# A Winograd convolution with batch norm and SiLU: readers of a bank swapped, and the last unit's copies and turns put in another order

## The chip, the core and the metric

The kernel runs on one core of a Trainium2 chip. The metric is the device time of one execution in microseconds (us). The kernel before takes 195.81 us, the median of 3 runs (195.16 to 196.03).

The engines have these names in the profile: PE is TensorE (matmuls, with its weight loads as PEld), DVE is VectorE, ACT is ScalarE, POOL is GpSimd, and SP is SyncE, which here only issues DMAs. A "q" behind a name (ACTq, SPq) is that engine's sequencer, for example while it issues a DMA. The accumulators of PE lie in eight banks of 512 fp32 columns by 128 partitions; the kernel holds them all as one tile, `ps_all`.

## The reference

The input x is (2, 2048, 1024), the weights w are (3, 1024, 1024), all in bfloat16. A convolution with three taps along the sequence is followed by a batch norm with given mean and variance, and by SiLU.

```python
K = 3
P = K // 2
S = x.shape[1]
xp = jnp.pad(x, ((0, 0), (P, P), (0, 0)))
y = sum(jnp.einsum('bsc,cd->bsd', xp[:, k:k + S, :], w[k]) for k in range(K))
inv_std = 1.0 / jnp.sqrt(var + 1e-5)
y = (y - mean) * (g * inv_std) + b
return _silu(y)
```

## The kernel before, in words

The convolution is done in Winograd form: six outputs at a time are worked out from eight input rows. A sequence of 2048 has 342 such tiles (`NTB`). There are three kinds of work.

**Transforms** (`transform`, L209). PE multiplies windows of x with a small constant matrix `Rm` (L216), which gives eight planes j of transformed input, already turned so that channels lie on partitions. ACT (L230) or DVE (L232) casts a group of two, three or four such results from banks of `ps_all` into `T_sb` in SBUF. A running estimate of each engine's load (`load`, `EVAC`) chooses which of the two casts a group.

**Weights** (`scale_weights`, `pair_weights`). POOL adds and subtracts the three taps to make the planes' weights, `uch` (L160 to L162); ACT scales copies of the taps by 2 and 4 for it (L148). Planes 0 and 7 use the raw taps, `wch`.

**Units** (`unit`, L251). A unit is 128 output channels of one batch: 16 units, of 8 channel blocks by 2 batches. For each of the eight planes, eight matmuls (`mms`, L241) add up 1024 input channels into one of four banks, called A, B, C and G. The planes come in the order 1, 3, 2, 4, 5, 7, 6, 0. Planes 1 and 2 go to bank A, 3 and 4 to B, 5 and 6 to C, 7 to G and 0 again to A. A second plane is added on top of the first, so the first must be copied out before: ACT copies plane 1 to `m1`, the sum of 1 and 2 to `s1`, plane 3 to `m3`, the sum of 3 and 4 to `s2`, plane 5 to `m5` (`copy_out`, L280). DVE builds the differences and the six outputs y0 to y5 with `scalar_tensor_tensor` (`stt`, L273, and one plain add, L305). The difference d1 is 2 m1 - A; the differences of the other two pairs are written over a bank: 2 m3 - B over bank B, 2 m5 - C over bank G. Units use the banks 0 to 3 and 4 to 7 by turns.

The order of the code around the change is:

```python
        yield from mms(bA, 2, dc, bi, c0, c1, False)
        copy_out(s1, A)
        stt(d1, m1, 2.0, A, op1=ALU.subtract)
        yield from mms(bB, 4, dc, bi, c0, c1, False)
        copy_out(s2, B_)
        for i in (2, 4):
            stt(y[i], B_, ALPHA * 2.0 ** i, s1)
        stt(B_, m3, 2.0, B_, op1=ALU.subtract)
```

Each engine does its instructions in the order in which the program emits them. Where two instructions touch the same bank from different engines, the one that was emitted later waits for the earlier one, also where both only read.

At the end of a unit three SiLU activations (L317) are not run but put on a list, `late`. They write `yT`, the outputs of the unit with channels on partitions. The next unit runs them between its own copies: `pace` (1, 0, 1, 1, 0) says how many of the list are taken off ahead of the copies m1, m3, s1, s2 and m5. So ACT's order in a unit is SiLU of y2 and y4, m1, m3, SiLU of y1, y3 and y5, s1, SiLU of y0, s2, m5. The scaling of weights comes behind m5. After that, `finish` turns the outputs back with one DMA transpose on SP's queue (`turn`, L386) and issues the stores of the unit before (`store_unit`, L400 and L404).

**Unit 0** is interleaved with the transforms of the second batch: every group of transforms is followed by two or three of the unit's matmuls. The unit has banks 0 to 3, the transforms go round banks 4 to 7. ACT and DVE do the casts of T_sb and the copies and differences of the unit in one stream. Plane 7 comes first in this unit.

**The last unit** (unit 15) is done in two parts, so that the end is short: columns 0 to 245 (`cut`) and then columns 245 to 342. Part one uses banks 4 to 7. Within it, after plane 7 (48 matmuls), PE turns the outputs of unit 14 itself (18 transposes, L446), and ACT copies them out to `o_before` (three copies, L469), which are stored from SP's queue. Part two uses banks 0 to 3. Behind it, PE turns part one's outputs in two blocks of 128 and 117 columns, which DVE copies to `o_end0` and `o_end1` (L478), and then part two's 97 columns in three steps, each behind its SiLU; DVE copies these to `o_end2` in two pieces (L486). Then come the stores: the parts of the blocks whose rows are a multiple of 16 on SP's queue, two small remainders of 30 and 2 rows of 128 elements on ACT's queue (`store_block`, L454 and L457).

Of the kernel before, what the change touches and what calls it, by code (L numbers as in the profile page):

```python
# [9 lines left out]
ALU = mybir.AluOpType  # L10
FP32 = mybir.dt.float32
BF16 = mybir.dt.bfloat16
# [15 lines left out]
ALPHA = -1.0 / 20.0  # L28
BETA = -4.0 / 5.0
M_OUT = 6  # L30
NJ = 8
WT = 21

# [2 lines left out]
def kernel(  # L36
# [10 lines left out]
    nc = tc.nc  # L47
    B, S, C = x.shape
    D = w.shape[2]
    P = 128  # L50
    CT = C // P
    DC = D // P
    assert S % P == 0 and C % P == 0 and D % P == 0
    NTB = (S + M_OUT - 1) // M_OUT
    assert NTB <= 512
    NWIN = (NTB + WT - 1) // WT

    NB = (NTB + P - 1) // P
# [46 lines left out]
    for k in range(NJ):  # L105
        j = 1
        while j < 7:
# [5 lines left out]
            while j1 + 1 < 7 and BT[j1 + 1][k] == v:  # L113
# [3 lines left out]
                out=Rm[:, j:j1 + 1, :],  # L117
# [4 lines left out]
                op1=ALU.add,  # L122
            )
            j = j1 + 1
    for j in (0, 7):
        for k in range(NJ):
            if BT[j][k] != 0:
                nc.gpsimd.affine_select(
                    out=Rm[:, j, :],
                    in_=Rm[:, j, :],  # L130
                    compare_op=ALU.not_equal,
                    fill=float(BT[j][k]),
                    base=-k,
                    pattern=[[-M_OUT, WT]],
                    channel_multiplier=1,
# [58 lines left out]
    epool = ctx.enter_context(tc.tile_pool(name="epool", bufs=1))  # L194
# [39 lines left out]
    def mms(bk, j, dc, bi, c0, c1, start):  # L234

        for ct in range(CT):
            if j in (0, 7):
                lhsT = raw[dc][0 if j == 0 else 2][:, ct, :]
            else:
                lhsT = wts[dc][:, j - 1, ct, :]  # L240
            nc.tensor.matmul(  # L241
                ps_all[:, bk * 512:bk * 512 + c1 - c0],
                lhsT=lhsT,
                rhs=T_sb[bi][:, ct, j, c0:c1],
                start=start and ct == 0,
                stop=ct == CT - 1,
                skip_group_check=not start,
            )
            yield

    def unit(dc, bi, c0, c1, banks, yT, late, pace=(1, 0, 1, 1, 0), seven_first=False):  # L251

        nn = c1 - c0  # L260
        A, B_, C_, G = [ps_all[:, k * 512:k * 512 + nn] for k in banks]
        bA, bB, bC, bG = banks
        pace = list(pace)

        def et(name):
            return epool.tile([P, NTB], FP32, name=name)[:, 0:nn]

        m1, m3, m5, s1, s2, d1 = (et(n) for n in ("m1", "m3", "m5", "s1", "s2", "d1"))
        y_all = epool.tile([P, M_OUT, NTB], FP32, name="y")[:, :, 0:nn]
        y = [y_all[:, i] for i in range(M_OUT)]  # L270

        def stt(o, i0, s, i1, op1=ALU.add):
            nc.vector.scalar_tensor_tensor(out=o, in0=i0, scalar=s, in1=i1, op0=ALU.mult, op1=op1)  # L273
            load["dve"] += 0.0013 * nn

        def copy_out(dst, src):
            for _ in range(pace.pop(0)):
                if late:
                    late.pop(0)()
            nc.scalar.copy(dst, src)  # L280
            load["act"] += 0.0013 * nn

        if seven_first:
            yield from mms(bG, 7, dc, bi, c0, c1, True)
        yield from mms(bA, 1, dc, bi, c0, c1, True)
        copy_out(m1, A)
        yield from mms(bB, 3, dc, bi, c0, c1, True)
        copy_out(m3, B_)
        yield from mms(bA, 2, dc, bi, c0, c1, False)
        copy_out(s1, A)  # L290
        stt(d1, m1, 2.0, A, op1=ALU.subtract)
        yield from mms(bB, 4, dc, bi, c0, c1, False)
        copy_out(s2, B_)
        for i in (2, 4):
            stt(y[i], B_, ALPHA * 2.0 ** i, s1)
        stt(B_, m3, 2.0, B_, op1=ALU.subtract)
        yield from mms(bC, 5, dc, bi, c0, c1, True)
        copy_out(m5, C_)
        while late:
            late.pop(0)()  # L300
        for i in (1, 3, 5):
            stt(y[i], B_, ALPHA * 2.0 ** i, d1)
        if not seven_first:
            yield from mms(bG, 7, dc, bi, c0, c1, True)
        nc.vector.tensor_tensor(y[5], G, y[5], op=ALU.add)  # L305
        yield from mms(bC, 6, dc, bi, c0, c1, False)
        for i in (2, 4):
            stt(y[i], C_, BETA * 0.5 ** i, y[i])
        stt(G, m5, 2.0, C_, op1=ALU.subtract)
        yield from mms(bA, 0, dc, bi, c0, c1, False)  # L310
        for i in (1, 3, 5):
            stt(y[i], G, BETA * 0.5 ** i, y[i])
        stt(y[0], s2, ALPHA, A)
        stt(y[0], C_, BETA, y[0])

        def silu(i0, i1):
            nc.scalar.activation(  # L317
                yT[:, i0:i1:2, c0:c1],
                y_all[:, i0:i1:2],
                ACT.Silu,  # L320
                bias=beta[:, dc:dc + 1],
                scale=sk[:, dc:dc + 1],
            )

        late.extend(lambda i=i: silu(*i) for i in ((2, 5), (1, 6), (0, 1)))

    def run(gen, n=None):
        while n is None or n > 0:
            if next(gen, run) is run:
                return  # L330
            if n is not None:
                n -= 1

    units = [(dc, bi) for dc in range(DC) for bi in range(B)]
    late = []
# [40 lines left out]
    endpool = ctx.enter_context(tc.tile_pool(name="endpool", bufs=1))  # L376
    out_f = out.flatten_outer_dims()
    FULL = S // M_OUT

    def rows(bi, n0, n1):  # L380
        r0 = bi * S
        return out_f[r0 + n0 * M_OUT:r0 + n1 * M_OUT]
# [9 lines left out]
    def store_unit(dc, bi, block):  # L392

        dcols = slice(dc * P, (dc + 1) * P)
        for nb in range(NB):
            n0, n1 = nb * P, min((nb + 1) * P, FULL)
            cuts = [n0, n1] if (n1 - n0) % 16 == 0 else [n0, n1 - (n1 - n0) % 16, n1]
            for a, z in zip(cuts, cuts[1:]):
                dst = rows(bi, a, z)[:, dcols].rearrange("(n i) d -> n i d", i=M_OUT)
                nc.sync.dma_start(out=dst, in_=block(nb)[a - n0:z - n0])  # L400
        if S % M_OUT:
            n0 = (NB - 1) * P
            dst = out_f[bi * S + FULL * M_OUT:(bi + 1) * S, dcols].rearrange("(n i) d -> n i d", i=S % M_OUT)
            nc.sync.dma_start(out=dst, in_=block(NB - 1)[FULL - n0:FULL - n0 + 1, 0:S % M_OUT])  # L404

    turned = []
# [8 lines left out]
    for ui, (dc, bi) in enumerate(units[1:-1], 1):  # L415
        yT = yTs[ui % 2]
# [17 lines left out]
    dc, bi = units[-1]  # L434
    yT = yTs[(len(units) - 1) % 2]
    half = 4 * ((len(units) - 1) % 2)
    here, there = [half + k for k in range(4)], [4 - half + k for k in range(4)]
    dcols = slice(dc * P, (dc + 1) * P)

    def turn_view(bk, at=0):  # L440
        pv = ps_all[:, bk * 512 + at:bk * 512 + at + M_OUT * P // 2]
        return pv.bitcast(BF16).rearrange("p (i d) -> p i d", d=P)
# [2 lines left out]
        for i in which:  # L445
            nc.tensor.transpose(pv[0:n1 - n0, i], yT[:, i, n0:n1], ident)  # L446

    def store_block(n0, n1, o_end):
        n2 = min(n1, FULL)
        n3 = n2 - (n2 - n0) % 16  # L450
        for a, z, queue in ((n0, n3, nc.sync), (n3, n2, nc.scalar)):
            if z > a:
                dst = rows(bi, a, z)[:, dcols].rearrange("(n i) d -> n i d", i=M_OUT)
                queue.dma_start(out=dst, in_=o_end[a - n0:z - n0])  # L454
        if n1 > FULL:
            dst = out_f[bi * S + FULL * M_OUT:(bi + 1) * S, dcols].rearrange("(n i) d -> n i d", i=S % M_OUT)
            nc.scalar.dma_start(out=dst, in_=o_end[FULL - n0:FULL - n0 + 1, 0:S % M_OUT])  # L457

    cut = FULL - (FULL // 16 // 4 + 1) * 16
    last = unit(dc, bi, 0, cut, here, yT, late)  # L460
    run(last, 48)
    while turned:
        store_unit(*turned.pop(0))
    o_before = endpool.tile([P, NB, M_OUT, P], BF16, name="o_before")
    for nb in range(NB):
        n0, n1 = nb * P, min((nb + 1) * P, NTB)
        pv = turn_view(there[nb], 512 - M_OUT * P // 2)
        turn_tiles(pv, yTs[len(units) % 2], n0, n1, (2, 4, 1, 3, 5, 0))
        nc.scalar.copy(o_before[0:n1 - n0, nb], pv[0:n1 - n0])  # L469
    run(last)  # L470
    store_unit(*units[-2], lambda nb: o_before[:, nb])
    run(unit(dc, bi, cut, NTB, there, yT, late))
    blocks = [(n, min(n + P, cut)) for n in range(0, cut, P)]
    ends = [endpool.tile([P, M_OUT, P], BF16, name=f"o_end{k}") for k in range(len(blocks) + 1)]
    for k, (n0, n1) in enumerate(blocks):
        pv = turn_view(here[k])
        turn_tiles(pv, yT, n0, n1, (2, 4, 1, 3, 5, 0))
        nc.vector.tensor_copy(ends[k][0:n1 - n0], pv[0:n1 - n0])  # L478
    pv = turn_view(here[3])
    nn = NTB - cut  # L480
    for which, done in (((2, 4), None), ((1, 3, 5), (1, 6)), ((0,), (0, 1))):
        late.pop(0)()
        turn_tiles(pv, yT, cut, NTB, which)
        if done:
            sl = slice(*done)
            nc.vector.tensor_copy(ends[-1][0:nn, sl], pv[0:nn, sl])  # L486
    for (n0, n1), o_end in zip(blocks, ends):
        store_block(n0, n1, o_end)
    store_block(cut, NTB, ends[-1])


# [28 lines left out]
```

## Time and profile before

| what | value |
|---|---|
| median of 3 runs | 195.81 us |
| the profiled execution | 196.92 us |
| its span, first to last instruction | 195.1 us |
| PE busy | 177.8 us (91%) |
| POOL busy | 164.7 us (84%) |
| DVE busy | 149.4 us (77%) |
| ACT busy | 124.2 us (64%) |
| mean granted clock of TensorE | 0.979 |
| matmuls of the units with `uch` (L241), 816 | 123.9 us, 299 ns each |
| matmuls of the units with `wch` (L241), 272 | 44.7 us, 303 ns each |
| matmuls of the transforms (L216), 272 | 31.8 us, 248 ns each |

The profile is of one execution. A share of busy time is a mean over stages that have different limits, so the stages have to be read one by one: the first batch's transforms up to some 22 us, unit 0 with the second batch's transforms up to some 42 us, units 1 to 14, the last unit from some 174 us on, and the stores at the end. Matmuls overlap in PE, so the duration of one is more than its share of time: eight of 342 columns start within 1.16 us.

In the rows of a timeline the first number is the start from the beginning of the span, the second the duration (of the whole row, where it holds several instructions, "x5"), then engine, line, operation, and what it writes and reads. In square brackets stands how long the engine had been idle before, and what ended that.

### The profile page before, as it was taken

What the parts mean: (1) busy time and instruction counts of PE and PEld (TensorE: products, weight loads), DVE (VectorE), ACT (ScalarE), POOL (GpSimd) and SP (SyncE); (2) the same over time, 40 slices, a digit from 0 to 9 for tenths busy, and PEclk for the clock granted to TensorE, in tenths of its full rate; (3) what the DMA queues carried; (4) which work ended last, traced back from release to release, by engine and by line L of the source; (5) the groups of instructions that cost most, each with busy time, mean ns of one, the idle gap of its engine ahead of it and who ended that gap; (6) DMA issues with size and microseconds to landing.
All of it is one profiled execution on the core that took longest, in us unless ns stands there. A gap on an engine that the chain in (4) does not pass through costs nothing.

```text
span 195.1 us, 3898 instructions
## 1 busy us (share of the span) xinstructions
PE 177.8 (91%) x1397; PEld 126.7 (65%) x1397; DVE 149.4 (77%) x345; ACT 124.2 (64%) x206; POOL 164.7 (84%) x105
## 2 busy tenths in 40 slices
PE   0779799989999999999999999999999999999840
PEld 0668588856666666666666666666666666679830
DVE  6369668996878696969696969686877878697880
ACT  3479558878378827873786287548736872827930
POOL 7899999999999999999999999999999999800000
PEclk9999879999999999999999999999999999999995
DMA  4999999900607487999292989774755657397505
GB/s 135 277 392 344 332 257 371 284 15 2 116 5 137 96 159 182 276 166 200 39 211 41 198 229 257 142 157 92 139 112 116 129 105 152 76 174 157 115 5 108
DMA packets 86823, 31.72 MB, mean 163 GB/s; under 512 B 73428, under 2 KB 82644, under 8 KB 86804
## 3 DMA queue, kind: packets, MB, share of 16 engines
q1 hardware_dynamic: 86637, 31.46, 69.8%
q8 instruction: 11, 0.18, 0.3%
q14 instruction: 8, 0.07, 0.1%
q0 software_dynamic: 128, 0.01, 0.0%
q10 hardware_dynamic: 39, 0.01, 0.0%
HBM read 14.82 MB, written 8.39 MB: 119 GB/s over the span
## 4 chain that ended last, share of the span: by engine, by line
PE 84%; DVE 7%; DMA 3%; SPq 2%; ACT 1%; issue 1%; DVEq 0%; ACTq 0%
PE ps_all L241 76%; PE ps_all L216 7%; DVE T_sb L232 4%; DMA xw<-in_x_dram 3%; DVE y L273 1%; SPq L206 1%; SPq L88 1%; PE ps_all L446 1%; DVE o_end L478 1%; DVE o_end L486 0%; ACT m L280 0%; ACT yT L317 0%; SPq L203 0%; SPq L202 0%; DVE ps_all L273 0%
## 5 line engine op out<-in xcount | busy, mean ns | idle before, releaser
L241 PE MATMUL ps_all<-T_sb,uch 128*128 128x342 bf16 (+2 forms) x816 | 123.9, 299 | 1.8 <-ACT m L280 1.8
L241 PEld LDWEIGHTS <-uch 128*128 128x128 bf16 x816 | 76.7, 97 | 34.5 <-issue 1.3
L317 ACT ACTIVATE yT<-y,beta,sk 128x684 bf16<-128x684 f32 (+8 forms) x51 | 47.1, 925 | 29.9 <-DVE y L273 29.8
L273 DVE SCALAR_TENSOR_TENSOR y<-ps_all,y 128x342 f32<-128x342 f32 (+2 forms) x102 | 45.4, 487 | 1.3
L241 PE MATMUL ps_all<-T_sb,wch 128*128 128x342 bf16 (+2 forms) x272 | 44.7, 303 | 0.1
L216 PE MATMUL ps_all<-Rm,xw 128*128 128x168 bf16 (+1 forms) x272 | 31.8, 248 | 8.5 <-DVE Rm L116 5.4
L280 ACT COPY m<-ps_all 128x342 f32<-128x342 f32 (+2 forms) x51 | 21.7, 427 | 20.6 <-PE ps_all L241 19.6
L230 ACT CAST T_sb<-ps_all 128x672 bf16<-128x672 f32 (+5 forms) x45 | 26.2, 606 | 13.0 <-PE ps_all L216 12.0
L216 PEld LDWEIGHTS <-xw 128*128 128x128 bf16 (+1 forms) x272 | 24.1, 104 | 14.9 <-POOL ident masks.py:199 5.4
L241 PEld LDWEIGHTS <-wch 128*128 128x128 bf16 x272 | 26.0, 98 | 11.6 <-DVE T_sb L232 0.3
L232 DVE CAST T_sb<-ps_all 128x672 bf16<-128x672 f32 (+3 forms) x40 | 26.1, 698 | 8.4 <-PE ps_all L216 8.2
L273 DVE SCALAR_TENSOR_TENSOR d<-m,ps_all 128x342 f32<-128x342 f32 (+2 forms) x17 | 8.3, 490 | 21.0 <-ACT s L280 21.0
L273 DVE SCALAR_TENSOR_TENSOR y<-ps_all,d 128x342 f32<-128x342 f32 (+2 forms) x51 | 22.0, 486 | 0.6
L273 DVE SCALAR_TENSOR_TENSOR y<-ps_all,s 128x342 f32<-128x342 f32 (+2 forms) x34 | 15.2, 489 | 6.3 <-ACT s L280 6.3
L161 POOL TENSOR_TENSOR uch<-e,w1x 128x1024 bf16<-128x1024 f32 x8 | 17.0, 2131 | 1.2 <-ACT w1x L148 0.7
L160 POOL TENSOR_TENSOR e<-wch 128x1024 f32<-128x1024 bf16 x8 | 17.0, 2125 | 0.8 <-DMA wch<-in_w_dram 0.8
L161 POOL TENSOR_TENSOR uch<-eh,w1x 128x1024 bf16<-128x1024 f32 x8 | 17.0, 2131 | 0.6
L161 POOL TENSOR_TENSOR uch<-e,wch 128x1024 bf16<-128x1024 f32 x8 | 17.0, 2129 | 0.6
L160 POOL TENSOR_TENSOR e<-wch,w2x 128x1024 f32<-128x1024 bf16 x8 | 17.0, 2125 | 0.3 <-ACT w2x L148 0.2
L160 POOL TENSOR_TENSOR eh<-w0x,wch 128x1024 f32<-128x1024 bf16 x8 | 17.0, 2124 | 0.1
L162 POOL TENSOR_TENSOR uch<-e,wch 128x1024 bf16<-128x1024 f32 x8 | 17.1, 2133 | 0.0
L162 POOL TENSOR_TENSOR uch<-eh,w1x 128x1024 bf16<-128x1024 f32 x8 | 17.1, 2132 | 0.0
(46 smaller groups left out, 113.6 us busy)
## 6 DMA issues: line engine op xcount, KB each, us to landing
xw<-in_x_dram SPq DMA_DIRECT2D x30, 256.0 KB
out_dram<-o_sb SPq DMA_DIRECT2D x28, 192.0 KB
wch<-in_w_dram SPq DMA_DIRECT2D x9, 512.0 KB
out_dram<-o_sb SPq DMA_DIRECT2D x14, 120.0 KB
wch<-in_w_dram SPq DMA_DIRECT2D x6, 256.0 KB
xw<-in_x_dram SPq DMA_DIRECT2D x2, 224.0 KB
out_dram<-o_before SPq DMA_DIRECT2D x2, 192.0 KB
o_sb<-yT SPq DMA_TRANSPOSE x14
```

The source lines that it names most:

```text
L88: nc.sync.dma_start(out=raw[dc][k], in_=w_all[:, k, :, dc * P:(dc + 1) * P])
L160: nc.gpsimd.tensor_tensor(e, a, c, op=ALU.add)
L161: nc.gpsimd.tensor_tensor(wts[dc][:, 2 * n], e, odd, op=ALU.add)
L162: nc.gpsimd.tensor_tensor(wts[dc][:, 2 * n + 1], e, odd, op=ALU.subtract)
L206: nc.sync.dma_start(out=xw[0:kk, :], in_=x[bi, t_lo:t_hi + 1, :])
L216: nc.tensor.matmul(banks[:, at:at + NJ * ntile], lhsT=xw[0:kk, (ct0 + c) * P:(ct0 + c + 1) * P], rhs=Rm[0:kk, :, 0:ntile], start=True, sto ...
L230: nc.scalar.copy(dst, src)
L232: nc.vector.tensor_copy(dst, src)
L241: nc.tensor.matmul(ps_all[:, bk * 512:bk * 512 + c1 - c0], lhsT=lhsT, rhs=T_sb[bi][:, ct, j, c0:c1], start=start and ct == 0, stop=ct == C ...
L273: nc.vector.scalar_tensor_tensor(out=o, in0=i0, scalar=s, in1=i1, op0=ALU.mult, op1=op1)
L280: nc.scalar.copy(dst, src)
L317: nc.scalar.activation(yT[:, i0:i1:2, c0:c1], y_all[:, i0:i1:2], ACT.Silu, bias=beta[:, dc:dc + 1], scale=sk[:, dc:dc + 1],)
```

## The change

In every unit, d1 is now emitted ahead of the copy s1 of the same bank, and y2 and y4 ahead of the copy s2 of the same bank. The tile of the six outputs y is split into three, one for each SiLU. In the last unit, part one takes one SiLU ahead of m3 and one ahead of s2 (`pace` 0, 1, 0, 1, 0) and the third behind m5. Unit 14 (the fifteenth) is turned by PE after 56 matmuls of part one, behind plane 6, not after 48. Two of the three copies to `o_before` follow at once; the third is put into the list between the SiLUs and so runs ahead of s1 in part two. The stores of unit 14 are issued after 33 matmuls of part two. Of the two blocks of part one, DVE copies only the first; ACT copies the second, behind the last SiLU. The stores are issued in another order, and on other queues: block one's 30 rows and its other rows on ACT's queue, the remainder of 2 rows on SP's. In the changed kernel all lines of `unit` stand one further down than before (L273 is L274, L280 is L281, L241 is L242).

```diff
+OUTPUTS = ((2, 4), (1, 3, 5), (0,))
...
-        y_all = epool.tile([P, M_OUT, NTB], FP32, name="y")[:, :, 0:nn]
-        y = [y_all[:, i] for i in range(M_OUT)]
+        groups = {g: epool.tile([P, len(g), NTB], FP32, name=f"y{g[0]}")[:, :, 0:nn] for g in OUTPUTS}
+        y = {i: t[:, k] for g, t in groups.items() for k, i in enumerate(g)}
...
         yield from mms(bA, 2, dc, bi, c0, c1, False)
+        stt(d1, m1, 2.0, A, op1=ALU.subtract)
         copy_out(s1, A)
-        stt(d1, m1, 2.0, A, op1=ALU.subtract)
         yield from mms(bB, 4, dc, bi, c0, c1, False)
-        copy_out(s2, B_)
         for i in (2, 4):
             stt(y[i], B_, ALPHA * 2.0 ** i, s1)
+        copy_out(s2, B_)
         stt(B_, m3, 2.0, B_, op1=ALU.subtract)
...
-        def silu(i0, i1):
+        def silu(g):
             nc.scalar.activation(
-                yT[:, i0:i1:2, c0:c1],
-                y_all[:, i0:i1:2],
+                yT[:, g[0]:g[-1] + 1:2, c0:c1],
+                groups[g],
...
-    last = unit(dc, bi, 0, cut, here, yT, late)
-    run(last, 48)
-    while turned:
-        store_unit(*turned.pop(0))
     o_before = endpool.tile([P, NB, M_OUT, P], BF16, name="o_before")
-    for nb in range(NB):
+
+    def turn_before(nb):
+
         n0, n1 = nb * P, min((nb + 1) * P, NTB)
         pv = turn_view(there[nb], 512 - M_OUT * P // 2)
         turn_tiles(pv, yTs[len(units) % 2], n0, n1, (2, 4, 1, 3, 5, 0))
-        nc.scalar.copy(o_before[0:n1 - n0, nb], pv[0:n1 - n0])
-    run(last)
+        return lambda: nc.scalar.copy(o_before[0:n1 - n0, nb], pv[0:n1 - n0])
+
+    first_part = unit(dc, bi, 0, cut, here, yT, late, pace=(0, 1, 0, 1, 0))
+    run(first_part, 56)
+    while turned:
+        store_unit(*turned.pop(0))
+    copies = [turn_before(nb) for nb in range(NB)]
+    run(first_part)
+    copies[0]()
+    copies[1]()
+    late.insert(1, copies[2])
+    last_part = unit(dc, bi, cut, NTB, there, yT, late, pace=(1, 0, 1, 1, 0))
+    run(last_part, 33)
     store_unit(*units[-2], lambda nb: o_before[:, nb])
-    run(unit(dc, bi, cut, NTB, there, yT, late))
+    run(last_part)
...
-    for k, (n0, n1) in enumerate(blocks):
-        pv = turn_view(here[k])
+    pvs = [turn_view(here[k]) for k in range(len(blocks))]
+    for pv, (n0, n1) in zip(pvs, blocks):
         turn_tiles(pv, yT, n0, n1, (2, 4, 1, 3, 5, 0))
-        nc.vector.tensor_copy(ends[k][0:n1 - n0], pv[0:n1 - n0])
+    nc.vector.tensor_copy(ends[0], pvs[0])
...
-    for (n0, n1), o_end in zip(blocks, ends):
-        store_block(n0, n1, o_end)
-    store_block(cut, NTB, ends[-1])
+    n0, n1 = blocks[1]
+    nc.scalar.copy(ends[1][0:n1 - n0], pvs[1][0:n1 - n0])
...
+    store_rows(nc.sync, 0, 0, P, ends[0])
+    store_rows(nc.sync, cut, cut, FULL, ends[2])
+    n2 = n1 - (n1 - n0) % 16
+    store_rows(nc.scalar, n0, n0, n2, ends[1])
+    dst = out_f[bi * S + FULL * M_OUT:(bi + 1) * S, dcols].rearrange("(n i) d -> n i d", i=S % M_OUT)
+    nc.sync.dma_start(out=dst, in_=ends[2][FULL - cut:FULL - cut + 1, 0:S % M_OUT])
+    if n2 < n1:
+        store_rows(nc.scalar, n0, n2, n1, ends[1])
```

More of the change, by code (lines that the diff above doesn't have):

```diff
@@ L323, in silu @@
             )
-        late.extend(lambda i=i: silu(*i) for i in ((2, 5), (1, 6), (0, 1)))
+        late.extend(lambda g=g: silu(g) for g in OUTPUTS)
     def run(gen, n=None):
@@ L446, in turn_tiles @@
             nc.tensor.transpose(pv[0:n1 - n0, i], yT[:, i, n0:n1], ident)
[L448 to L457, printed above, removed]
     cut = FULL - (FULL // 16 // 4 + 1) * 16
-    last = unit(dc, bi, 0, cut, here, yT, late)
-    run(last, 48)
-    while turned:
-        store_unit(*turned.pop(0))
     o_before = endpool.tile([P, NB, M_OUT, P], BF16, name="o_before")
-    for nb in range(NB):
+    def turn_before(nb):
         n0, n1 = nb * P, min((nb + 1) * P, NTB)
@@ L486, with store_rows @@
             nc.vector.tensor_copy(ends[-1][0:nn, sl], pv[0:nn, sl])
-    for (n0, n1), o_end in zip(blocks, ends):
-        store_block(n0, n1, o_end)
-    store_block(cut, NTB, ends[-1])
+    n0, n1 = blocks[1]
+    nc.scalar.copy(ends[1][0:n1 - n0], pvs[1][0:n1 - n0])
+    def store_rows(queue, n0, a, z, o_end):
+        dst = rows(bi, a, z)[:, dcols].rearrange("(n i) d -> n i d", i=M_OUT)
+        queue.dma_start(out=dst, in_=o_end[a - n0:z - n0])
+    store_rows(nc.sync, 0, 0, P, ends[0])
[6 more added lines that the diff above has]
+        store_rows(nc.scalar, n0, n2, n1, ends[1])
 _INS = ['x', 'w', 'mean', 'var', 'g', 'b']
```

## The prediction

> **What bounds the kernel now.** I read the chain of work that ended last first, then the same chain in order of time, then the table of waits.
>
> ```profile
> PE 84%; DVE 7%; DMA 3%; SPq 2%; ACT 1%; issue 1%; DVEq 0%; ACTq 0%
> ```
>
> ```profile
> 40.74 0.25 PE ps_all L216 x3
> ...
> 41.29 0.35 ACT m L280
> ...
> 42.59 137.20 PE ps_all L241 x958
> 179.79 1.00 PE ps_all L446 x18
> ```
>
> ```profile
> DVE d L273 <- ACT s L280: 21.0, 17, 1.8
> ...
> PE ps_all L241 <- ACT m L280: 1.8, 3, 0.8
> ```
>
> The chain is TensorE (84%). From 42.6 to 182 us it has no gap: eight matmuls of 342 columns take 1.16 us and a unit of 64 takes 9.29. The 21.0 us in which the difference d1 waits for the copy s1 are DVE's own, and free. Work can be won or lost in three places only: before 42.6 us, where unit 0 is interleaved with the second batch's transforms and one copy (m5) already holds PE for 0.71 us; after 179.6 us; or in the middle, if a new wait makes a copy late for PE.
>
> **Unit 0, first swap.** Before, the ACT rows of this stretch are:
>
> ```profile
> 35.61 0.45 ACT L280 COPY s<-ps_all 128x342 f32<-128x342 f32 x1
> 35.94 0.94 ACT L230 CAST T_sb<-ps_all 128x504 bf16<-128x504 f32 x2
> ...
> 38.43 0.45 ACT L280 COPY s<-ps_all 128x342 f32<-128x342 f32 x1
> 38.76 2.53 ACT L230 CAST T_sb<-ps_all 128x336 bf16<-128x336 f32 x5
> 41.19 0.45 ACT L280 COPY m<-ps_all 128x342 f32<-128x342 f32 x1
> ```
>
> and the DVE rows:
>
> ```profile
> 36.09 0.51 DVE L273 SCALAR_TENSOR_TENSOR d<-m,ps_all 128x342 f32<-128x342 f32 x1 [0.17 <-ACT s L280]
> 36.52 2.48 DVE L232 CAST T_sb<-ps_all 128x504 bf16<-128x504 f32 x4
> 38.92 0.93 DVE L273 SCALAR_TENSOR_TENSOR y<-ps_all,s 128x342 f32<-128x342 f32 x2
> 39.76 0.51 DVE L273 SCALAR_TENSOR_TENSOR ps_all<-m,ps_all 128x342 f32<-128x342 f32 x1
> ```
>
> Between them stands what both engines really do here: T_sb casts, nearly back to back, that free the banks which PE's next transforms (L216) write. The two readers of a bank are ordered as emitted, so after the change s1 waits for d1 and s2 for y2 and y4, and each cast queued behind a copy on ACT waits with it. Hand-overs are read off the rows: 0.03 us from ACT to DVE (s1 ends 36.06, d1 starts 36.09), 0.05 us to PE (m5 ends 41.64, PE goes on at 41.69); back to back, ACT starts 0.11 us and DVE 0.08 us before its previous row ends.
>
> DVE's cast ahead of d1 runs from 35.41 for 0.51, so d1 starts at 35.84 instead of 36.09 and ends at 36.35. s1 starts at 36.38 instead of 35.61. The cast behind it moves from 35.94 to 36.71 and ends at 37.32. The transform that reuses its bank ran at 36.73 and now starts at 37.37: **PE is held 0.64 us**. Part is made up by pauses, and some 0.48 stays: DVE's last cast ahead of y2 waits for PE and moves from 38.32 to 38.80.
>
> **Unit 0, second swap.** y2 then starts at 39.39 and y4 ends at 40.32 (0.93 for both). s2 starts at 40.36 instead of 38.43. Behind it stand five casts and m5, in 2.76 us from s2 to m5 (41.19 less 38.43), or 2.60 without the pauses for PE at their end. m5 starts at 42.96, ends at 43.41, and the matmul that waits for it starts at 43.46 instead of 41.69: **+1.77 us**. This holds the 0.64 and the old 0.71 in it. PE then runs without a gap, so nothing gives it back. Lower bound: without the first step y4 ends at 39.85 as now, s2 starts at 39.88, m5 at 42.48, +1.29. Upper bound: 1.93, the whole move of s2. I take 1.77, worked from the rows themselves.
>
> **Units 1 to 14.** In the unit at 128 us, s2 is at 133.11, m5 at 134.21, and the matmul that needs m5 at 135.12. After, d1 runs at 131.95, when PE is done with the bank (133.11 less the 1.16 of eight matmuls), 0.7 us earlier than now; s1 at 132.50; y2 and y4 from 133.11 to 134.04; s2 at 134.08, m5 at 134.41, done at 134.85. PE would find it ready 0.22 us early. Cost 0, hidden by TensorE; if that cover went it would cost what m5 is late, 14 times. The in-place difference on bank B moves from 134.43 to 134.55, DVE has over 0.4 us to spare per unit, and the next unit starts level. POOL, its weights (PE reads the last 2 us after they are ready) and SP's order are untouched. The three y tiles hold the same elements as the one tile; I cost them at nothing, since SiLU(2,4) already starts 0.04 us after its y4.
>
> **The last unit** (times as if PE entered it at 174.58, as now). In part one ACT runs m1, SiLU(2,4), m3, s1, SiLU(1,3,5) of 1.24 us, s2, m5: s2 waits to 179.61 and m5 to 179.89 (now 179.04). Plane 6's matmuls now precede the 18 turns that covered them (179.63 to 180.63), so PE waits for m5 until 180.30. Plane 0 follows the turns at 182.15, not 181.48: +0.67. The o_before copies start at 181.67 instead of 180.16 and ACT runs without pause (two copies, SiLU, m1, m3, third copy, s1, SiLU(1,3,5), s2, m5) to the last m5 at 186.19, now 185.52: PE's plane 6 is +0.66. DVE, whose bank-B difference now waits for s2, ends its last y at 189.16, now 188.83.
>
> The end is stores:
>
> ```profile
> 189.55 2.01 SPq L454 DMA_DIRECT2D out_dram<-o_end  x3
> ...
> 190.02 2.37 ACTq L454 DMA_DIRECT2D out_dram<-o_end  x1
> ...
> 192.48 0.63 ACTq L457 DMA_DIRECT2D out_dram<-o_end  x1
> ```
>
> DVE loses one block copy of 0.55, so its last copy ends at 190.85 instead of 190.94. But block 0 is copied 0.33 later, and its store issues at 189.88, now 189.55. The 504 KB of the three blocks flow from 190.75 to 193.50 at a DMA share of 0.94, so a start 0.33 later ends them at 193.83, against the last bytes now 0.64 after the issue that ends at 193.11, about 193.75: +0.1. Block 1 is copied on ACT at 189.63 in 0.80 (the o_before row) and issued there from 190.47. If ACT's issue again takes 2.37, a 0.85 one of 30 rows behind it ends at 193.8: +0.7. If two queues moved bytes faster, block 2's store, issued at 190.88, would set the end: 1.2 to its first byte and 0.7 for its bytes, -0.8. I take **+0.3** for the tail, nearest to the row in which ACT's issue was slow, partly hidden.
>
> The Trainium skill's "DMA: Bandwidth & Descriptors", section "Issuing engines are not separate DMA queues", says that issuing from several engines saves only the sequencer's time, because all run on the same 16 DMA engines; by it the tail lies between +0.1 and +0.7 and the gain of 0.8 is not there. The share of 0.94 speaks for that, though no run here has the bytes on two queues.
>
> **Sum.** The profiled execution took 196.92 (span 195.14 and 1.78 around it): 196.92 + 1.77 + 0.3 = 199.0. Its time is 1.11 above the median of the runs, and the sum does not hang on that, so 195.81 + 2.07 = **197.9 us**.
>
> **Rivals.** *The clock falls* (0.20). The granted clock went to half for one stretch after PE was little busy:
>
> ```profile
> 19.84:23.25 3.41, 2.20 (x28) 1.57 (x26) 2.29 (x5) 2.02 (x4) 3.33 (x3) 1.00 1.05 360
> 23.25:26.67 3.42, 3.42 (x22) 2.75 (x21) 1.88 (x3) 1.42 (x3) 3.26 (x3) 0.50 1.08 220
> ...
> 40.32:43.73 3.41, 2.69 (x23) 1.59 (x22) 3.27 (x8) 2.44 (x6) 3.17 (x2) 1.00 0.01 2
> ```
>
> The second column is PE busy and the third from last the clock. 2.20 of 3.41 us was followed by half clock, 2.69 was not. With the new holds the stretch from 40.32 has some 2.0: below the one that fell. Half clock for 3.41 us costs 1.7: 199.6. It depends on where the stretches lie in each execution; only about a third of the places contain all the holds. The Trainium skill's "TensorE: Matmul & The Clock Gate", section "What's actually happening", wants a whole idle window of about 3.4 us before the clock drops; by it this rival costs 0, but the first row was 2.20 busy and dropped.
>
> *The casts' delay is hidden* (0.08). If PE had more spare banks than the rows show, unit 0 costs about 0 and the tail alone remains: 195.0 to 196.5, say 196.0. Against it: PE follows the cast that frees its bank by 0.18 us only.
>
> *The tail wins* (0.06). With unit 0 hidden, two queues must carry the stores at once; from a store end over 1 us earlier it is faster: some 194.8. For it: DVE loses 0.55 of copies and ACT's two late issues shrink. Against: the bytes already fill the DMA engines.
>
> *The middle breaks* (0.06). If m5 is over 0.22 late in each unit, say by 0.2, 14 x 0.2 = 2.8 comes on top: 200.7.
>
> **How the numbers follow.** My forecast has 0.60 and by itself reaches from 195.81 + 1.29 - 0.8 = 196.3 to 195.81 + 1.93 + 0.7 = 198.4. With the clock case added (199.6, and as much run spread as the runs show) the range is 196.4 to 199.8, leaving out under 2 in 10. A measurement tells about 0.5% (0.98 us) from no change. Slower by more: 0.57 of the forecast's 0.60, the clock and the middle, 0.83. Within: the hidden case and the forecast's low edge, 0.11. Faster: 0.06.
>
> **What would show it.** Right: s<-ps_all waits for DVE in the waits; the gap of PE for m5 near 43 us; s2 of unit 0 at about 40.4; the 958-matmul piece starting 1.8 later, and no PE wait for m between 45 and 175 us. In the tail, a PE wait for m5 before the turns, DVE's last copy at the same distance from that piece as now, ACT's first store issue over 0.7 us. Wrong: the long piece starting at 42.6 as now, or gaps inside it, or half clock near 44 us (the second case).

## The result, and the profile after

The changed kernel takes 199.12 us, the median of 17 runs (197.04 to 202.02). The kernel before, run beside it, takes 196.32 us, the median of 17 (195.16 to 197.66). The ratio is 1.0103, with an interval of 1.007 to 1.0136: slower by 1.0%. The forecast, 197.9 to 195.81, was a ratio of 1.0107. Five of the 17 runs after, all over 200 us, show a lower mean clock (0.969 to 0.977) and are not in the ratio.

The profiled execution took 199.12 us, with a span of 197.3 us and a mean clock of 0.988. The chain of work that ended last, by engine, in the page after:

```profile
PE 76%; DVE 11%; ACT 4%; DMA 2%; SPq 2%; issue 2%; DVEq 0%; ACTq 0%
```

PE had 84% before. This is a share of the chain, not time that PE lost: PE can be busy while the chain runs over another engine. The part of it that lies in unit 0 stands in the same chain in order of time (start, duration, what):

```profile
35.27 0.42 DVE d L274
35.72 0.45 ACT s L281
...
38.81 0.85 DVE y L274 x2
...
39.69 0.45 ACT s L281
...
42.38 0.46 ACT m L281
42.84 0.04 issue
42.88 0.31 PE ps_all L242
...
43.78 111.26 PE ps_all L242 x766
...
155.04 16.43 PE ps_all L242 x112
```

The order of the readers has turned round. DVE's differences now lead the copies, and the copies lead the casts (not shown) and m5. From 43.78 to 171.47 us PE works almost without a break; the one step out of that is at 155.04. Behind 171.47 the chain runs mostly over DVE and ACT, where before it stayed on PE until 183.20; the larger part of the lost share lies there. The table of waits says the same of the readers:

```profile
ACT s L281 <- DVE y L274: 10.4, 15, 1.3
...
DVE d L274 <- PE ps_all L242: 7.0, 14, 1.0
...
PE ps_all L242 <- ACT m L281: 2.0, 4, 0.7
...
ACT s L281 <- DVE d L274: 1.9, 3, 1.1
```

Before, d1 waited 21.0 us for s1 and no copy waited for DVE. Now the copies wait 12.3 us (10.4 and 1.9), and d1 waits for PE alone. None of that is PE's time by itself: PE waits for m copies 2.0 us in all, 1.8 before. The ACT rows of unit 0 after show where a wait becomes PE's:

```profile
35.72 0.45 ACT L281 COPY s<-ps_all 128x342 f32<-128x342 f32 x1 [0.64 <-DVE d L274]
36.06 2.29 ACT L231 CAST T_sb<-ps_all 128x504 bf16<-128x504 f32 x4
39.69 0.45 ACT L281 COPY s<-ps_all 128x342 f32<-128x342 f32 x1 [1.34 <-DVE y L274]
40.03 2.01 ACT L231 CAST T_sb<-ps_all 128x336 bf16<-128x336 f32 x4
42.21 0.28 ACT L231 CAST T_sb<-ps_all 128x144 bf16<-128x144 f32 x1 [0.17 <-PE ps_all L217]
42.38 0.45 ACT L281 COPY m<-ps_all 128x342 f32<-128x342 f32 x1
```

ACT stands idle for 0.64 and 1.34 us, and the casts and m5 behind it are late.

The starts of two traces can't be set side by side without a common point, because the transforms of the first batch end sooner in one execution than in another. The start of the copy m3 of unit 0 is such a point: it lies ahead of both swaps. Here it is, with the matmul that waits for m5, before and then after:

```profile
32.62 0.45 ACT L280 COPY m<-ps_all 128x342 f32<-128x342 f32 x1
41.69 0.30 PE L241 MATMUL ps_all<-T_sb,uch 128*128 128x342 bf16 x1 [0.71 <-ACT m L280]
```

```profile
31.96 0.45 ACT L281 COPY m<-ps_all 128x342 f32<-128x342 f32 x1
42.88 0.31 PE L242 MATMUL ps_all<-T_sb,uch 128*128 128x342 bf16 x1 [0.71 <-ACT m L281]
```

So after had 0.66 us in hand. Counted from m3, s1 starts 0.77 us later than before, s2 1.92 and m5 1.85. From there every trace can be cut in four: to the matmul that waits for m5 in unit 0; from there to PE's first matmul of the last unit; to the end of DVE's last copy; to the end of the span. In us, for all kernels of this study:

| kernel | m3 to PE going on | to the last unit | to DVE's last copy | to the end |
|---|---|---|---|---|
| before | 9.07 | 132.89 | 16.36 | 4.20 |
| after | 10.92 | 133.06 | 16.29 | 5.03 |
| after, unit 0 in old order | 9.08 | 133.06 | 16.28 | 5.04 |
| before, unit 0 swapped | 10.91 | 134.34 | 16.39 | 5.05 |
| before, unit 0, second swap | 10.46 | 134.42 | 16.39 | 5.05 |
| before, units 1 to 14 swapped | 9.07 | 136.29 | 16.66 | 4.20 |
| the same with three y tiles | 9.08 | 133.05 | 16.52 | 4.14 |
| after, old order everywhere | 9.07 | 132.89 | 15.72 | 5.03 |
| the same, block 1 stored by SP | 9.09 | 132.88 | 15.72 | 5.12 |
| before, block 0 copied by ACT | 9.08 | 132.88 | 15.93 | 3.97 |
| the same, copies first | 8.99 | 132.89 | 16.73 | 3.90 |
| the same, three y tiles | 9.10 | 132.88 | 15.63 | 4.01 |

After against before: 1.85 in unit 0, 0.17 in the middle, -0.07 in the last unit and 0.83 in the stores make 2.78; less the 0.66 in hand, that is 2.12, the difference of the spans (197.26 less 195.14). The first three columns repeat to 0.1 us wherever the same code runs at full clock; the last one does not, which is taken up below.

### The profile page after: what moved, and what is told of

Same layout as the page of the kernel before. It is cut to its first block, busy times and chain, and to the rows that moved or that the text cites. A ratio compares the mean times of both kernels' runs of the same rounds, so it can differ in the third digit from the quotient of the medians.

```text
span 197.3 us, 3897 instructions
## 1 busy us (share of the span) xinstructions
PE 178.7 (91%) x1397; PEld 127.4 (65%) x1397; DVE 150.6 (76%) x344; ACT 125.6 (64%) x207; POOL 164.7 (84%) x105
## 4 chain that ended last, share of the span: by engine, by line
PE 76%; DVE 11%; ACT 4%; DMA 2%; SPq 2%; issue 2%; DVEq 0%; ACTq 0%
PE ps_all L242 69%; PE ps_all L217 6%; DVE T_sb L233 5%; DVE y L274 4%; DMA xw<-in_x_dram 2%; ACT s L281 1%; SPq L207 1%; ACT T_sb L231 1%; SPq L89 1%; DVE ps_all L274 1%; ACT yT L318 1%; ACT o_before L457 1%; ACT m L281 0%; DVE d L274 0%; DVE y L306 0%
## 5 line engine op out<-in xcount | busy, mean ns | idle before, releaser
L242 PE MATMUL ps_all<-T_sb,uch 128*128 128x342 bf16 (+2 forms) x816 | 124.1, 299 | 2.0 <-ACT m L281 2.0
L242 PEld LDWEIGHTS <-uch 128*128 128x128 bf16 x816 | 76.8, 97 | 35.3 <-issue 1.9
L274 DVE SCALAR_TENSOR_TENSOR y<-ps_all,y 128x342 f32<-128x342 f32 (+2 forms) x102 | 45.4, 487 | 1.7 <-PE ps_all L242 0.5
L242 PE MATMUL ps_all<-T_sb,wch 128*128 128x342 bf16 (+2 forms) x272 | 43.8, 300 | 0.1
L217 PEld LDWEIGHTS <-xw 128*128 128x128 bf16 (+1 forms) x272 | 25.3, 108 | 15.3 <-issue 5.5
L242 PEld LDWEIGHTS <-wch 128*128 128x128 bf16 x272 | 25.6, 97 | 11.6 <-DVE T_sb L233 0.3
L281 ACT COPY m<-ps_all 128x342 f32<-128x342 f32 (+2 forms) x51 | 21.9, 430 | 13.9 <-PE ps_all L242 13.9
L274 DVE SCALAR_TENSOR_TENSOR ps_all<-m,ps_all 128x342 f32<-128x342 f32 (+2 forms) x34 | 16.8, 493 | 9.7 <-ACT s L281 9.7
L281 ACT COPY s<-ps_all 128x342 f32<-128x342 f32 (+2 forms) x34 | 14.5, 427 | 14.2 <-DVE y L274 10.4
L274 DVE SCALAR_TENSOR_TENSOR y<-ps_all,s 128x342 f32<-128x342 f32 (+2 forms) x34 | 15.2, 488 | 10.2 <-PE ps_all L242 9.4
L274 DVE SCALAR_TENSOR_TENSOR y<-ps_all,d 128x342 f32<-128x342 f32 (+2 forms) x51 | 22.0, 487 | 0.5
L162 POOL TENSOR_TENSOR uch<-e,wch 128x1024 bf16<-128x1024 f32 x8 | 17.0, 2128 | 0.6
```

What stands on the lines that cost most here:

```text
L162: nc.gpsimd.tensor_tensor(wts[dc][:, 2 * n], e, odd, op=ALU.add)
L217: nc.tensor.matmul(banks[:, at:at + NJ * ntile], lhsT=xw[0:kk, (ct0 + c) * P:(ct0 + c + 1) * P], rhs=Rm[0:kk, :, 0:ntile], start=True, sto ...
L242: nc.tensor.matmul(ps_all[:, bk * 512:bk * 512 + c1 - c0], lhsT=lhsT, rhs=T_sb[bi][:, ct, j, c0:c1], start=start and ct == 0, stop=ct == C ...
```

## The experiments

All were timed beside the kernel before. The ratios have intervals of 0.3 to 0.6% (0.6 to 1.2 us) either way, so the rows of the table carry more than the ratios do.

### Unit 0 put back

The changed kernel, with copy first in unit 0 alone:

```diff
-        stt(d1, m1, 2.0, A, op1=ALU.subtract)
-        copy_out(s1, A)
+        if not seven_first:
+            stt(d1, m1, 2.0, A, op1=ALU.subtract)
+            copy_out(s1, A)
+        else:
+            copy_out(s1, A)
+            stt(d1, m1, 2.0, A, op1=ALU.subtract)
...
+        if not (not seven_first):
+            copy_out(s2, B_)
         for i in (2, 4):
             stt(y[i], B_, ALPHA * 2.0 ** i, s1)
-        copy_out(s2, B_)
+        if not seven_first:
+            copy_out(s2, B_)
```

> The changed kernel with the old order of both readers (copy first) in unit 0 alone; everything else as changed. My theory: unit 0's hold on TensorE was worth 1.77 us between the two traces, so the matmul that waits for m5 comes back to the place it has in the kernel before, TensorE's wait for m5 in unit 0 falls from its present size to about 0.7 us less the first hold, and what remains is the tail's 0.75 us and 0.17 us in the middle: 0.9 us above the kernel before, ratio 1.003 to 1.006. Rival, the tail and the middle carry the loss: ratio stays at 1.009 to 1.011. Rival, the fallen clock carries it: the ratio falls below 1.003 only in runs of full clock and TensorE keeps its new place.

Measured: ratio 1.0049 (1.0013 to 1.0084). The first column is back at 9.08, 1.84 less than after; middle and end are those of the changed kernel. My theory holds: unit 0 carries about half of what the change costs by the ratios, two thirds (1.84 of 2.78) by the rows, and the rest is still there.

### Both swaps, and the second alone, in unit 0 alone

The kernel before, with `if seven_first:` around the new order.

> The kernel before with both swaps in unit 0 alone. My theory: plus 1.77 us, ratio 1.009, s2 of unit 0 1.9 us later after its transform phase, m5 1.8 us later, and the rest of the trace level with the kernel before. Rival, TensorE has spare banks and the hold is absorbed: ratio within 0.998 to 1.002. Rival, the clock falls after the hold: in profiles and runs where it does, another 1.7 us (ratio 1.017).

> The kernel before with the second swap alone (y2 and y4 ahead of s2) in unit 0 alone. My theory: the casts queued behind s2 on ACT move with it, the matmul that waits for m5 is 1.29 us later (the prediction's lower bound for unit 0), ratio 1.006 to 1.007, and the first swap accounts for the other 0.48. Rival, the second swap alone already costs the whole 1.77 because s2 waits for the pair y2 and y4 whatever came before: m5 1.77 later, ratio 1.009. Rival, hidden: level, ratio 1.000.

Measured: with both, ratio 1.0115 (1.0057 to 1.0172), first column +1.84. With the second alone, first column +1.39, where 1.29 was expected and the rival had 1.77, and ratio 1.0144 (1.0082 to 1.0205), more than either theory of that kernel gave. The first swap so accounts for 0.45, by difference; it was not run by itself. The casts' delay is not hidden: that rival falls.

Another rival came in here: both profiles show TensorE at half clock behind the new hold. These are stretches of the kernel with both swaps; columns: stretch, its length, busy time of PE, PEld, DVE, ACT, POOL with counts, the granted clock, DMA share, GB/s:

```profile
40.47:43.88 3.41, 1.71 (x16) 1.02 (x14) 2.65 (x7) 2.98 (x7) 3.11 (x2) 1.00 0.03 8
43.88:47.29 3.41, 3.41 (x15) 1.58 (x15) 1.63 (x4) 2.42 (x4) 0.80 (x1) 0.50 0.03 7
```

and of the kernel with the second swap alone:

```profile
40.05:43.46 3.41, 1.77 (x15) 1.02 (x14) 2.65 (x7) 2.98 (x7) 3.26 (x3) 1.00 0.02 6
43.46:46.87 3.41, 3.41 (x16) 1.74 (x16) 1.73 (x5) 2.42 (x4) 1.28 (x2) 0.50 0.03 7
```

PE was busy for 1.71 and 1.77 of 3.41 us, and the next 3.41 us went at half clock. The second column of the table gives the price: 134.34 and 134.42 against 132.89, so 1.45 and 1.53 us. The ratio of the second kernel can't be understood without it: its interval is 1.6 to 4.0 us, above 1.39 alone, and holds 1.39 and 1.53 together. That of the first, 1.1 to 3.4 us, holds its 1.84 with or without the clock.

In the profile of the changed kernel the stretches lie otherwise and the clock holds. It falls there only at 192.38 us, behind PE's last matmul; counted back from that point in steps of 3.413 us, the stretches around the hold are:

```profile
38.78:42.20 3.42, 2.40 (x22) 1.53 (x21) 2.66 (x7) 2.35 (x5) 3.27 (x3) 1.00 0.39 102
42.20:45.61 3.41, 2.73 (x21) 1.62 (x20) 2.85 (x7) 2.70 (x6) 1.72 (x2) 1.00 0.03 7
```

The same holds are there, but the border of two stretches cuts them.

### Units 1 to 14 alone, with one y tile and with three

The kernel before, with the new order where the unit is neither unit 0 nor a part of the last (first kernel), and the same with y split as in the change (second).

```diff
+        groups = {g: epool.tile([P, len(g), NTB], FP32, name=f"y{g[0]}")[:, :, 0:nn] for g in OUTPUTS}
+        y = {i: t[:, k] for g, t in groups.items() for k, i in enumerate(g)}
```

> The kernel before with both swaps in units 1 to 14 alone (unit 0 and both parts of the last unit as before). My theory: m5 stays ahead of TensorE by some 0.24 us in each unit, so 0 to 0.2 us, ratio 0.999 to 1.002, with no wait of TensorE for m between 45 and 175 us but for a stray one. Rival, the middle breaks: 0.2 us in each of 14 units, plus 2.8 us, ratio 1.014.

> The kernel before with both swaps in units 1 to 14 and with y in three tiles, as the change has it; unit 0 and the last unit in the old order. My new theory, from the run with the swaps but one y tile (a unit of 9.53 instead of 9.29 us, in which y2 waits for SiLU(0) of the unit before): the one tile makes y2 wait for the last SiLU that reads any part of it; with three tiles y2 waits only for TensorE and SiLU(2,4), a unit is back at 9.29 us, ratio 0.999 to 1.002. Rival, the swaps themselves break the middle and the changed kernel is saved by something else (its unit 0 or its last unit): the ratio stays near 1.02 and the wait of y2 for the SiLU stays in the table of waits.

Measured: 1.0211 (1.0161 to 1.0261) with one tile, so my first theory fell for this kernel and the rival was right in kind, though it had said 1.014; 1.0016 (0.9983 to 1.0049) with three. The second column says 136.29 and 133.05: one tile costs 3.40 us more than before, 0.24 in each of 14 units; three tiles cost 0.16. The waits of the kernel with one tile:

```profile
DVE y L273 <- ACT yT L324: 15.1, 14, 1.1
ACT s L280 <- DVE y L273: 14.8, 14, 1.1
```

Those of the one with three:

```profile
DVE y L274 <- PE ps_all L242: 9.4, 14, 1.0
ACT s L281 <- DVE y L274: 9.1, 14, 1.0
```

With one tile, y2 waits for a SiLU, in 14 units of 14. The rows of one unit, ACT first and then DVE, show which:

```profile
124.66 0.45 ACT L280 COPY s<-ps_all 128x342 f32<-128x342 f32 x1
125.00 0.67 ACT L324 ACTIVATE yT<-y,beta,sk 128x342 bf16<-128x342 f32 x1
126.73 0.45 ACT L280 COPY s<-ps_all 128x342 f32<-128x342 f32 x1 [1.06 <-DVE y L273]
127.07 0.45 ACT L280 COPY m<-ps_all 128x342 f32<-128x342 f32 x1
```

```profile
125.70 0.94 DVE L273 SCALAR_TENSOR_TENSOR y<-ps_all,s 128x342 f32<-128x342 f32 x2 [1.08 <-ACT yT L324]
```

The SiLU of a single output (128x342) that ends at 125.67 is SiLU(0) of the unit before. It reads y0, y2 writes y2, but the two lie in one tile with one buffer, and the writer waits for the tile's last reader. Then comes a chain that no engine's busy share shows: d1, s1, SiLU(0), y2 and y4, s2, m5, and m5 ends at 127.52. PE's next matmul into that bank starts at 127.57, and a unit takes 9.53 us instead of 9.29. In the old order s2 stood between SiLU(0) and y2 anyway, so the single tile cost nothing.

### The last unit without the swaps, and block 1's store on SP

The changed kernel with copy first in every unit; and this with one word changed in the stores.

```diff
-    store_rows(nc.scalar, n0, n0, n2, ends[1])
+    store_rows(nc.sync, n0, n0, n2, ends[1])
```

> The changed kernel with the old order of both readers in every unit: only the last unit's new order, the three y tiles and the new stores are left. My theory from the two traces: the last unit costs 0.75 us after TensorE enters it, so plus 0.5 to 0.8 us, ratio 1.002 to 1.005; the prediction's term was 0.3 (1.0015), with bounds -0.8 to 0.7. Rival, the tail's loss comes from the swapped readers in the last unit's two parts (s2 waits for y2 and y4, and m5 behind it holds TensorE 0.40 us before plane 6): then this kernel is within 0.1 us of the kernel before, or faster, ratio 0.998 to 1.001.

> The changed kernel with the old order of both readers in every unit and with the 672-row store of block 1 on SP's queue instead of ACT's. In all traces with the changed stores the end comes 4.97 to 4.98 us after DVE's last copy, in those with the old stores mostly 4.09 to 4.15. Theory A: the second queue and ACT's slow issues cost this; on SP's queue the distance falls to 4.2 to 4.5 us, 0.5 to 0.8 us better than the same kernel with the store on ACT, ratio to the kernel before 0.997 to 1.000. Theory B: the later start of the first store costs it (0.96 instead of 1.44 us ahead of the last copy's end), because the bytes of all three fill the DMA engines: the distance stays at 4.8 to 5.1 us, ratio 1.001 to 1.004.

Measured: 1.0018 (0.9987 to 1.0049) and 1.0009 (0.9971 to 1.0046). The last unit's new order, with one block copy less on DVE, brings DVE's last copy 0.64 us nearer (15.72 against 16.36); the swapped readers take 0.57 of it away again (16.29). My rival for the first kernel put that on the last unit's two parts alone. But the kernel with units 1 to 14 swapped and three tiles, whose last unit has the old order, has 16.52, so 0.16 of the 0.57 may come from the units ahead; the swaps in the last unit alone were not run. What is left of the loss lies behind the last copy: 5.03 against 4.20. By the rows the first kernel is so 0.19 us slower than before (0.83 less 0.64), nearer to the rival than to my 0.5 to 0.8. The expectation counted from a point 0.05 later, hence its 4.97 to 4.98 and 4.09 to 4.15.

With all big stores on SP's queue it is 5.12, so theory A, the second queue, falls. The issues of the two kernels after their start differ, the end doesn't. In the changed kernel:

```profile
191.26 1.62 SPq L491 DMA_DIRECT2D out_dram<-o_end  x2
192.93 0.70 SPq L498 DMA_DIRECT2D out_dram<-o_end  x1
```

```profile
191.81 2.11 ACTq L491 DMA_DIRECT2D out_dram<-o_end  x2
```

The first store starts at 191.26 with the last copy ending at 192.23, 0.97 ahead; before it was 189.55 to 190.94, 1.39 ahead. That fits theory B for 0.42 us of the 0.83. The two kernels with only unit 0 changed have the old stores, start the first 1.42 ahead and still need 5.05. So the old stores end in 4.14 to 4.20 us in three profiles and in 5.05 in two, and the new ones in 5.03 to 5.12 in four. The stores cost between 0.5 us (the means, 5.06 less 4.53) and 0.83.

The DMA share shows where the two kernels differ. Here is the stretch in which the bytes of the stores move, and the one from the last byte to the end, before and then after (the last two columns are DMA share and GB/s):

```profile
190.78:193.79 3.01, 0.00 (x0) 0.00 (x0) 0.16 (x1) 0.00 (x0) 0.00 (x0) 0.50 0.87 174
193.79:195.14 1.35, 0.00 (x0) 0.00 (x0) 0.00 (x0) 0.00 (x0) 0.00 (x0) 0.50 0.00 0
```

```profile
192.48:195.58 3.10, 0.00 (x0) 0.00 (x0) 0.00 (x0) 0.00 (x0) 0.00 (x0) 0.50 0.88 169
195.58:197.25 1.67, 0.00 (x0) 0.00 (x0) 0.00 (x0) 0.00 (x0) 0.00 (x0) 0.50 0.00 0
```

Counted from DVE's last copy, the last byte moves at 2.85 us before and at 3.35 after: 0.50 of the 0.83, and 0.42 of this is the later start of the bytes. In the five profiles with old stores that point lies at 2.54 to 2.97, in the four with new ones at 3.27 to 3.51, so this part separates them. The other 0.33 comes behind the last byte. That stretch is 1.35 us long before, 2.09 in the two kernels with only unit 0 changed and 1.60 to 1.75 in the other nine profiles, whichever stores they have; why it varies is not shown.

### Toward a faster version: block 0 on ACT, copies first, three tiles

ACT waited 1.84 us ahead of its last three SiLUs in the kernel before, while DVE copied two blocks behind its last y.

```diff
-        nc.vector.tensor_copy(ends[k][0:n1 - n0], pv[0:n1 - n0])
+        (nc.vector.tensor_copy if k else nc.scalar.copy)(ends[k][0:n1 - n0], pv[0:n1 - n0])
```

The second kernel adds `pace=(1, 0, 0, 0, 0)` to part two of the last unit; the third adds the three y tiles to that.

> The kernel before with the copy of block 0 of the last unit on ACT, ahead of its last three SiLUs, where ACT waits 1.84 us, instead of on DVE. My theory of the tail: its end is set by the issue of the stores, one after the other, and by their bytes; so block 0's store starts some 1.6 us earlier, the last copy of DVE some 0.4 us earlier, and the end comes 0.5 to 1.0 us earlier, ratio 0.995 to 0.998. Rival, the SiLUs behind the copy on ACT are late by its 0.8 us and with them the last block: 0 to 0.3 us slower, ratio 1.000 to 1.002.

> The kernel before with block 0's copy on ACT and, in part two of the last unit, the copies s1, s2 and m5 ahead of SiLU(1,3,5) and SiLU(0) of part one on ACT. My theory: TensorE's wait of 0.80 us for m5 goes and DVE's last y ends 0.6 to 0.9 us earlier, on top of the copy's gain, so 1.0 to 1.8 us faster, ratio 0.991 to 0.995. Rival, the two SiLUs that now come later hold the turns of the first blocks, and these hold the rest: no faster than with block 0's copy alone.

> The kernel before with y in three tiles, block 0's copy on ACT and, in part two of the last unit, s1, s2 and m5 ahead of SiLU(1,3,5) and SiLU(0); the old order of the readers everywhere. The run without the three tiles lost its gain to a wait of y2 for those two SiLUs (1.64 us in the DVE rows). My theory: as in the middle units, three tiles take that wait away, so y2 of part two starts some 1.3 us earlier, DVE's last copy ends about 15.0 us after TensorE enters the last unit instead of 16.4 before (15.9 with block 0's copy alone), and the kernel is 1.2 to 1.8 us faster than before, ratio 0.991 to 0.994. Rival, the wait is for ACT itself and not for the tile (the SiLUs only happen to run there): y2 waits as before, ratio 0.999 to 1.002. Rival, TensorE's turns of the first blocks, which need the late SiLUs, take the place of the wait: last copy at 15.7 or later, ratio 0.996 to 0.998.

Measured: 0.9969 (0.994 to 0.9998), 1.0013 (0.9982 to 1.0045) and 0.9923 (0.9894 to 0.9951). The first gains 0.43 up to the last copy and 0.23 behind it, as expected. The second loses it; that is the rival's number, but not mainly by the turns that the rival named. The copies did come earlier, and PE's waits for m fell from 1.8 to 1.0 us, but y2 met the tile again:

```profile
185.28 0.43 DVE L273 SCALAR_TENSOR_TENSOR y<-ps_all,s 128x97 f32<-128x97 f32 x2 [1.64 <-ACT yT L317]
```

In the third this wait is gone, and a smaller one, of y1 for SiLU(1,3,5) in their own tile, is left:

```profile
184.56 0.41 DVE L274 SCALAR_TENSOR_TENSOR y<-ps_all,s 128x97 f32<-128x97 f32 x2
184.89 0.25 DVE L274 SCALAR_TENSOR_TENSOR ps_all<-m,ps_all 128x97 f32<-128x97 f32 x1
185.80 0.59 DVE L274 SCALAR_TENSOR_TENSOR y<-ps_all,d 128x97 f32<-128x97 f32 x3 [0.65 <-ACT yT L318]
```

The rival that the wait is ACT's own, and not the tile's, falls. DVE's last copy is at 15.63, not at the 15.0 expected: after the 0.65, ACT's last three SiLUs run back to back from 187.26, right behind block 0's copy, and set the pace, so the rival that the late SiLUs hold the end is partly right. Its profile adds up to 0.9 us less than before behind m3 (0.73 to the last copy, 0.19 behind it); the ratio gives 1.5 us, 1.0 to 2.1; where the rest comes from is not shown. It is 0.8% faster than the kernel before, against which the changed one was 1.0% slower, and has the three tiles of the change, but none of its swaps.

## Why the prediction was right, and where it was off

- **What bounds the kernel** was right: PE's chain, and three places at which it can be touched.
- **Unit 0** was right in mechanism and nearly in size. The prediction gave 1.77 (0.48 and 1.29); the traces give 1.85 (0.45 and 1.39). The steps agree too: s1 was forecast 0.77 later, s2 1.93 and m5 1.77, and they are 0.77, 1.92 and 1.85 later. It was the largest term, and putting it back took it away.
- **Units 1 to 14** cost 0.17 and not 0. The margin by which m5 is done ahead of PE was forecast at 0.22 and is 0.24 in all of them but unit 12. There y2 starts at 153.18 us although s1 ended at 152.65 and PE's last matmul into the bank at 152.72, some 0.36 later than elsewhere. Of that 0.19 is covered (the 0.24 less 0.05 for the hand-over to PE), and 0.17 is left. The kernels with unit 0 in old order, and with units 1 to 14 swapped and three tiles, lose the same 0.16 to 0.17 in the same unit; what makes y2 late there was not found.
- **The step "I cost them at nothing"**, of the three y tiles, is the one that failed as reasoning. It was right for the sum, since the tiles are in the change, but wrong in what they are for: the prediction worked out when PE and s1 let y2 start, and left out that the y tile itself must be free. By the run with one tile, its rival "the middle breaks" would have been the result without the split, at 3.40 us where it said 2.8.
- **The last unit and the stores** came to 0.76, not 0.3. The mis-sized term is that of the stores. DVE's last copy was forecast 0.09 early and is 0.07 early. Behind it the prediction put 0.1 for later bytes and up to 0.7 for ACT's slow issue, and took 0.3 for all. The profiles show 0.83: 0.50 in later bytes, and 0.33 behind the last byte, a stretch for which the prediction had no term. The upper bound of 0.7 was 0.06 too low. The reason that it leaned on, ACT's slow issue, is not the cause: ACT's two issues were done at 193.92, counted in the unit 1.2 us earlier than the bound assumed, and with the big one on SP the end is no earlier.
- **The clock** did not fall in the profiled execution while PE had work, but it is no empty rival: it fell in the two profiles with the same hold in unit 0 and there cost 1.45 to 1.53 us, where 1.7 was forecast. How often it fell in executions of the changed kernel that were not profiled is not shown. The mean clock can't tell: it takes in the half clock behind PE's last matmul too, which alone makes the 0.988 of the profile after.
- **The tail wins** and **the delay is hidden** both fell. The prediction's sum, 2.07 on the median, stands against 2.0 by the ratio (1.0103 of 196.32) and 2.78 by the rows. The ratio's interval, 1.4 to 2.7, just misses the rows, mostly through the stores. That the sum meets the ratio to 0.1 us is in part luck: by the rows each of its terms, unit 0, the middle and the stores, was too small, by 0.7 us together.

## What to carry to other kernels

Where two engines read the same buffer and are ordered as emitted, the engine of the second reader pays, and with it all that is queued behind; so put first the reader whose engine has the most waited-for work behind it. In unit 0 that was the copy on ACT, whose next casts and m5 TensorE needs. A tile with one buffer is held by its last reader, whatever part of it that reads: before moving a writer ahead, look at who still reads any of the tile, or split it. And compare traces from a common point, stage by stage: a whole span hides a gain of 0.64 and a loss of 0.57 in the same stage.

## What the runs showed of the hardware

In every trace here the granted clock changes, within the span, only at points that lie multiples of 3.41 us apart; with the second swap alone in unit 0 these are 22.98, 26.40, 43.46 and 46.88 us. In the traces, stretches in which PE was busy for 1.71 and 1.77 us were followed by half clock. At the end of the first batch's transforms each of the twelve profiles has a less busy stretch: half clock followed the five with 2.18 to 2.20 us, and not the seven with 2.22 to 2.70. Yet busy time alone does not decide it, since in the last unit full clock followed one with 1.85, here in the changed kernel with unit 0 in old order:

```profile
185.05:188.46 3.41, 1.85 (x30) 1.56 (x29) 2.63 (x13) 2.14 (x7) 0.00 (x0) 1.00 0.22 43
188.46:191.88 3.42, 0.58 (x4) 0.34 (x4) 1.24 (x3) 1.12 (x3) 0.00 (x0) 1.00 0.46 91
```

The Trainium skill's "TensorE: Matmul & The Clock Gate", section "What's actually happening", speaks of a whole idle window; none of these seven stretches, behind which the clock fell, was idle.

Issuing a store of the last unit's blocks took 0.58 to 0.70 us on SP and between 0.62 and 2.37 us on ACT, but moving the 672-row one from ACT to SP moved the end by 0.09 us only, and to the later side. That agrees with the section "Issuing engines are not separate DMA queues" of the Trainium skill's "DMA: Bandwidth & Descriptors", which the prediction set against a gain from two queues.
